# A gated recurrence's output written feature by feature, in quarters of the matmul array

## The chip, the cores and the metric

The kernel runs on one core of a Trainium2 chip. The metric is the device time of one execution in microseconds. A core has a matmul engine (TensorE, PE in the profile, with PEld for its weight loads), three engines for elementwise work (VectorE = DVE, ScalarE = ACT, GpSimd = POOL), and queues from which transfers are issued (SP's above all). Matmul results go to PSUM, in banks of 512 fp32 columns; all else is in SBUF, with 128 partitions.

## The reference

Two stages. The first is a recurrence over 768 time steps for 4 batches and 8 heads of 48 features; the second is a feed-forward layer (MLP) on its output.

```python
f = 1.0 / (1.0 + np.exp(-f_logit))
for t in range(S):
    state = f[:, :, t, :, None] * state + np.einsum('bhd,bhe->bhde', k[:, :, t], v[:, :, t])
    y[:, :, t] = np.einsum('bhd,bhde->bhe', q[:, :, t], state)
x = y.transpose(0, 2, 1, 3).reshape(B * S, H * D)      # 3072 x 384
g = x @ w_gate                                         # 384 x 1536
out = (g / (1 + np.exp(-g)) * (x @ w_val)) @ w_out     # 1536 x 384
```

All inputs and the output are fp32 at the reference; the weights lie in memory as 64-bit floats, which the kernel converts itself.

## The kernel before

Time is cut into NCH = 6 blocks of C = 128 steps. A *unit* is one batch in one block, so there are 24 units, block by block with the four batches inside. Within a unit the recurrence is turned into matmuls. `attention(u)` (line 496) is a generator whose steps are:

- step 0: sigmoid of f, transposed so that features lie on partitions. Heads go in pairs: pair `a` of four has its two heads (`par` 0 and 1) at partitions 0 and 64. In blocks 0 and 1 the transposes are matmuls with an identity (line 505, tiles fTp, kTp, qTp); from block 2 on VectorE does them (lines 511, 531, 532).
- step 1: products of the gates from each step to the block's end (`tail`, a scan on VectorE, line 519), and three small operations.
- step 2: kT scaled by the tails, a second scan (`head`), qT scaled by it (lines 537 to 540), and from block 1 on `decayed`, the carried state times the whole block's decay (line 544), at the end of the step.
- step 3: scores `sc` = k against q (line 552), made causal on VectorE into `A` (line 554); the transpose `kt` of kT (line 559).
- step 4: the output y, and `dS`, the block's addition to the state (line 606), which the last block leaves out.
- step 5: in block 0 alone, the transposes of the output.

The MLP wants its input as `xT`: 384 features in three columns of 128 partitions, 512 tokens (four batches of one block) in the free dimension. Before the change step 4 gets there in two ways. In block 0 y comes out with time on partitions (line 599, eight matmuls), ScalarE copies it to `x`, three transposes (line 619) and a copy (line 620) make `xT`. In blocks 1 to 5 y comes out transposed at once, one head to a half of the array (64 columns): eight matmuls with `decayed` (line 578, 48 rows and 64 columns each) and eight with v and `A` (line 582, 128 rows and 64 columns) into two PSUM banks. Two ScalarE copies make `yT` (line 586), and ten transfers from SBUF to SBUF on SP's queue (line 593) move each head's 48 features to its place in `xT`, ten because heads 2 and 5 straddle two columns of 128.

The MLP has two forms. Block 0's (`mlp_plain`) is done directly, while the weights are loaded in 18 pieces, sized on ScalarE and joined on VectorE (lines 447 to 459). Blocks 1 to 5 (`mlp_fifteen`, `down_seven`) use fewer products with sums made on VectorE; ScalarE copies products out of PSUM (line 841).

What sets the order of the work: block 0's four units run first, in an order written out by hand at the end of `short_path` (`run(b, steps)`), which is kept on TensorE, VectorE and ScalarE. Before them `keep_warm(n)` puts n matmuls on dummy data. Then, for each block c, `take_turns` weaves the pieces of the MLP of block c with the steps of the units of block c + 1 (`attention_steps`); within that a scheduler places each instruction in its engine's queue ahead of time, by its own costs, and each engine runs its queue in order. SP's queue, in order too, carries the loads of f, k, q, v (`load`, two units ahead in blocks 0 and 1 and one ahead later, `load_after`), the weight pieces (`fetches`) and the transfers to `xT`. From block 1 on `later` has three PSUM banks, which go round among sc (two), kt, y (two) and dS.

## Time and profile before

| | us |
|---|---|
| median of 8 executions | 634.02 (632.58 to 635.73) |
| the profiled execution | 633.93 |
| its span | 632.2 |
| TensorE busy | 616.2 (97%) |
| VectorE busy | 500.3 (79%) |
| ScalarE busy | 288.7 (46%) |
| y in blocks 1 to 5: L578, L582 busy (320 instructions each) | 16.3, 23.6 |
| y and its transposes in block 0: L599, x12 transposes of L619 | 7.8, about 0.27 each |
| copies of yT (40) | 14.4 |
| transfers yT to xT (200) | 1.8 each from issue to landing |

The profile records each instruction of one execution with its start, its length and what it waited for. Every fp32 matmul shows as two instructions, each with its weight load. Successive matmuls overlap, so a matmul's length is more than what it adds; the distance between starts is what it adds. Rows of a group give line, engine, operation, output<-inputs, shapes and count; a bracket names the idle time before an instruction and what ended it. The chain of waits follows the work that ended last back through what released it. "issue" is time in which an engine waited for nothing that the profile shows; a letter q after an engine (SPq) means its queue. A stretch's row gives the busy time of each engine between two times and the matmul clock that was granted in it (1.0 is full).

### The profile page before, as it was taken

The numbers are of one execution on the slowest core, as the hardware profiler recorded it, in microseconds if no ns is written. First come the engines' busy times: TensorE is split into PE (matmuls) and PEld (weight loads), VectorE is DVE, ScalarE is ACT, GpSimd is POOL, SyncE is SP. The second block draws the span as 40 slices with busy tenths as digits, with TensorE's granted clock in tenths as the row PEclk, the third lists the DMA queues.
The fourth block names the chain that finished last, engine by engine and source line by source line (L and its number), as shares of the span: only waits on it lengthen the run. The fifth ranks groups of instructions, "written<-read, shape, count | busy, mean of one in ns | idle before, by whom it ended". The sixth has DMA issues, their size and how long they took to land.

```text
span 632.2 us, 10566 instructions
## 1 busy us (share of the span) xinstructions
PE 616.2 (97%) x3894; PEld 498.7 (79%) x3894; DVE 500.3 (79%) x941; ACT 288.7 (46%) x528; POOL 2.9 (0%) x22
## 2 busy tenths in 40 slices
PE   7999999999998999999999999999999999999996
PEld 4954545666777789888889988889988889988896
DVE  5888879968899999579997579998669992557641
ACT  1474655403764731476641265562175540166600
POOL 1000000000000000000000000000000000000000
PEclk8999999999998999999999999999999999999999
DMA  9997474106133122422323402323312210100001
GB/s 176 215 215 231 145 193 137 49 14 178 45 86 97 51 51 53 132 60 64 78 72 86 113 25 70 82 58 91 111 43 51 62 26 8 61 0 1 0 1 54
DMA packets 98395, 51.89 MB, mean 82 GB/s; under 512 B 56864, under 2 KB 92192, under 8 KB 98336
## 3 DMA queue, kind: packets, MB, share of 16 engines
q1 hardware_dynamic: 95024, 46.63, 31.2%
q10 hardware_dynamic: 3312, 4.52, 2.0%
q8 instruction: 32, 0.52, 0.4%
q14 instruction: 27, 0.22, 0.1%
HBM read 42.47 MB, written 4.72 MB: 75 GB/s over the span
## 4 chain that ended last, share of the span: by engine, by line
PE 84%; DVE 7%; DMA 3%; ACT 2%; SPq 2%; issue 2%; DVEq 0%; ACTq 0%
PE o L934 17%; PE A L836 14%; PE B L836 11%; PE gate L666 5%; PE val L666 5%; PE o L690 5%; PE o L836 4%; PE c L836 4%; PE sc L552 4%; PE y L582 3%; PE o L988 3%; PE y L578 2%; PE kt L559 1%; PE dS L606 1%; DVE c L731 1%
## 5 line engine op out<-in xcount | busy, mean ns | idle before, releaser
L934 PE MATMUL o<-w_out,h 128*128 128x192 f32 x360 | 62.6, 330 | 0.6 <-DVE h L853 0.3
L836 PE MATMUL A<-xs,w_both 128*128 128x256 f32 x240 | 62.9, 384 | 0.1
L841 ACT COPY c<-A 128x512 f32<-128x512 f32 x40 | 23.5, 587 | 84.3 <-PE A L836 74.3
L934 PEld LDWEIGHTS o<-w_out,h 128*128 128x128 f32 x360 | 58.1, 190 | 2.5 <-ACT c L951 1.1
L728 DVE TENSOR_TENSOR c<-c,aside 128x512 f32<-128x512 f32 x60 | 41.7, 696 | 18.5 <-ACT aside L841 17.8
L841 ACT COPY aside<-A 128x512 f32<-128x512 f32 x60 | 35.1, 584 | 38.1 <-PE A L836 38.1
L836 PEld LDWEIGHTS A<-xs,w_both 128*128 128x128 f32 x240 | 45.5, 192 | 6.9 <-ACT aside L841 0.4
L853 DVE TENSOR_TENSOR h<-h,c 128x256 f32<-128x256 f32 x100 | 42.2, 433 | 8.2 <-ACT h L852 8.2
L731 DVE TENSOR_TENSOR c<-c,aside 128x512 f32<-128x512 f32 x60 | 41.9, 698 | 2.1 <-ACT aside L841 1.8
L836 PE MATMUL B<-xT,extra 128*128 128x256 f32 x160 | 41.8, 384 | 1.3 <-ACT aside L841 1.2
L852 ACT ACTIVATE h<-c 128x256 f32<-128x256 f32 x100 | 41.7, 419 | 2.1 <-DVE c L728 1.5
L836 PE MATMUL c<-xT,w_both 128*128 128x256 f32 x160 | 42.0, 385 | 0.0
L836 PE MATMUL B<-xs,w_both 128*128 128x256 f32 x160 | 41.8, 384 | 0.0
L836 PE MATMUL A<-xs,extra 128*128 128x256 f32 x160 | 41.1, 379 | 0.0
L934 PE MATMUL o<-ws,h 128*128 128x192 f32 x240 | 41.0, 327 | 0.0
L841 ACT COPY aside<-B 128x512 f32<-128x512 f32 x60 | 35.0, 584 | 10.7 <-PE B L836 10.5
L731 DVE TENSOR_TENSOR c<-o,c 128x512 f32<-128x512 f32 x40 | 27.7, 693 | 14.8 <-PE o L836 13.3
L934 PEld LDWEIGHTS o<-ws,h 128*128 128x128 f32 x240 | 39.1, 190 | 0.2
L554 DVE TENSOR_TENSOR A<-sc,causal 128x512 f32<-128x512 f32 x48 | 31.1, 686 | 5.8 <-PE sc L552 5.8
L836 PEld LDWEIGHTS B<-xT,extra 128*128 128x128 f32 x160 | 29.9, 191 | 6.6 <-ACT aside L841 2.4
L586 ACT COPY yT<-y 128x256 f32<-128x256 f32 x40 | 14.4, 373 | 44.3 <-PE y L582 37.3
L552 PEld LDWEIGHTS sc<-qT,kT 48*128 48x128 f32 x384 | 24.7, 187 | 12.5 <-issue 6.4
(132 smaller groups left out, 1196.8 us busy)
## 6 DMA issues: line engine op xcount, KB each, us to landing
fsquares<-in_f_logit_dram SPq DMA_DIRECT2D x64, 96.0 KB, 2.4
ksquares<-in_k_dram SPq DMA_DIRECT2D x64, 96.0 KB, 2.4
qsquares<-in_q_dram SPq DMA_DIRECT2D x64, 96.0 KB, 2.4
v<-in_v_dram SPq DMA_DIRECT2D x24, 192.0 KB, 3.8
w<-in_moe_w_gate_dram SPq DMA_DIRECT2D x6, 768.0 KB, 4.7
w<-in_moe_w_val_dram SPq DMA_DIRECT2D x6, 768.0 KB, 5.3
w<-in_moe_w_out_dram SPq DMA_DIRECT2D x6, 768.0 KB, 5.0
out_dram<-ob ACTq DMA_DIRECT2D x23, 192.0 KB, 2.6
```

The source lines that it names most:

```text
L552: nc.tensor.matmul(sc[par][:, a * C:(a + 1) * C], lhsT=kT[r, a, :], rhs=qT[r, a, :], start=True, stop=True)
L554: nc.vector.tensor_tensor(A[:, par], sc[par].rearrange("p (a t) -> p a t", t=C), causal.unsqueeze(1).broadcast_to((128, HP, C)), ALU.mult)
L582: nc.tensor.matmul(place(a, par), lhsT=v_[:, 2 * a + par, :], rhs=A[:, par, a, :], start=False, stop=a >= HP - 2, skip_group_check=True)
L666: nc.tensor.matmul(p, lhsT=w[:, i, j * 128:(j + 1) * 128], rhs=xT[c][:, i, :], start=(i == 0), stop=(i == KT - 1))
L690: nc.tensor.matmul(p, lhsT=h[n // 2][:, n % 2 * 2 + b // 2, b % 2 * C:(b % 2 + 1) * C], rhs=w_out[:, j, :], start=(n == 0), stop=(n == NF ...
L728: nc.vector.tensor_tensor(dst, a, b, ALU.add)
L731: nc.vector.tensor_tensor(dst, a, b, ALU.subtract)
L836: nc.tensor.matmul(p[name][:, n, :], lhsT=weights_of[a][:, n, cols], rhs=tokens[b], start=fresh and n == 0, stop=True, skip_group_check=True)
L841: nc.scalar.copy(t, p[name])
L852: nc.scalar.activation(dst, src[:, 0, :], AF.Silu)
L853: nc.vector.tensor_tensor(dst, dst, src[:, 1, :], ALU.mult)
L934: nc.tensor.matmul(p[:, n, :], lhsT=lhsTs[j][:, n * C:(n + 1) * C], rhs=rhs[:, j, :], start=first and j == 0 and n == 0, stop=j == NP - 1, ...
```

## The change

The output now comes out of TensorE in the places that `xT` wants, for every block. The 384 features are 12 pieces of 32. Piece n goes to partitions 32 (n mod 4) onwards, that is to one quarter of the array's columns, and to column n // 4 of one PSUM bank. Three pieces hold a pair of heads (96 features). For the carried state `decayed` is copied by ScalarE (two copies, one for each head of a pair) into `blocks`, a tile with two 48 x 48 blocks on the diagonal and zeros elsewhere, so that one matmul of 128 rows and 32 columns serves each piece. For v, with zeros behind each head's 48 features, `flat` lets a slice of 32 features begin 16 before a head or run 16 past it; a piece that two heads share gets two matmuls. One copy then makes `xT`. The product `decayed` moves ahead of kT's scaling. Step 5 is gone, the transfers to `xT` are gone, and y takes one bank.

With it goes another order of loads at the start: f, k, q of two units, then v of the first; v of each later unit with the loads two ahead; one weight piece with each of the first three units. The warming matmuls before the first scores are 6 instead of 12.

```diff
-    decayed = const.tile([128, HP, W], FP32, tag="decayed", name="decayed")
+    decayed = const.tile([128, HP, D], FP32, tag="decayed", name="decayed")
+    blocks = const.tile([128, HP, 2 * D], FP32, tag="blocks", name="blocks")
+    nc.gpsimd.memset(blocks, 0.0)
...
+        if c:
+            nc.vector.tensor_tensor(decayed, states[b], whole.broadcast_to((128, HP, D)), ALU.mult)
+            for par in range(2):
+                r = rows_of(par)
+                nc.scalar.copy(blocks[r, :, par * D:(par + 1) * D], decayed[r])
         nc.vector.tensor_tensor(kT, kp, pairs(tail, 2)[:, :, 0:C], ALU.mult)
...
-        if c:
-            if c < SQUARES:
-                load_after(u)
-            nc.vector.tensor_tensor(decayed[:, :, 0:D], states[b], whole.broadcast_to((128, HP, D)), ALU.mult)
+        if 0 < c < SQUARES:
+            load_after(u)
...
+        y = bank("y")
+
+        def place(n):
+            return y[Q * (n % 4):Q * (n % 4) + Q, n // 4 * C:(n // 4 + 1) * C]
+
+        per = 2 * D // Q
         if c:
-            y = [bank("y") for _ in range(2)]
...
-            for a in range(HP):
-                for par in range(2):
-                    r = rows_of(par)
-                    nc.tensor.matmul(place(a, par), lhsT=decayed[r, a, :], rhs=qT[r, a, :],
-                                     start=a < 2, stop=False, skip_group_check=True)
-            for par in range(2):
-                for a in range(HP):
-                    nc.tensor.matmul(place(a, par), lhsT=v_[:, 2 * a + par, :], rhs=A[:, par, a, :],
-                                     start=False, stop=a >= HP - 2, skip_group_check=True)
-            yT = att.tile([128, 2, HP // 2 * C], FP32, tag="x", name="yT")
...
-                    nc.sync.dma_start(out=xT[c][f % 128:f % 128 + n, f // 128, b * C:(b + 1) * C],
-                                      in_=yT[r:r + n, par, a // 2 * C:(a // 2 + 1) * C])
...
+            for n in range(DM // Q):
+                nc.tensor.matmul(place(n), lhsT=blocks[:, n // per, n % per * Q:(n % per + 1) * Q], rhs=qT[:, n // per, :],
+                                 start=n < 4, stop=False, skip_group_check=True)
+        flat = v_.rearrange("t h e -> t (h e)")
+        met = {n % 4 for n in range(DM // Q)} if c else set()
+        for par in range(2):
+            for n in range(DM // Q):
+                h = 2 * (n // per) + par
+                at = n * Q - h * D
+                if -Q < at < D:
+                    nc.tensor.matmul(place(n), lhsT=flat[:, W * h + at:W * h + at + Q], rhs=A[:, par, n // per, :],
+                                     start=n % 4 not in met, stop=par == 1 or at + Q <= D, skip_group_check=True)
+                    met.add(n % 4)
+        nc.scalar.copy(xT[c][:, :, b * C:(b + 1) * C], y[:, 0:DM].rearrange("p (a t) -> p a t", t=C))
...
-        if not c:
-            p = bank("xTp")
-            for i in range(KT):
-                nc.tensor.transpose(p[:, i * C:(i + 1) * C], x[:, i * 128:(i + 1) * 128], ident)
...
-        parts = [1, 2, 1, 2]
+        parts = [1, 2, 1, 1]
...
-        load(u)
+        load(u, "fkq")
+    load(0, "v")
...
+    def load_ahead(u):
+
+        if u + NRAW < B:
+            load(u + NRAW, "fkq")
+            load(u + 1, "v")
+        elif u + 1 < B:
+            load(u + 1, "v")
+        if u + 1 < B:
+            fetches.pop(0)()
+        if u + NRAW >= B:
+            load(u + NRAW)
...
-    load_after(0)
+    load_ahead(0)
...
-            keep_warm(12)
+            keep_warm(6)
...
-        load_after(b)
-        if b == 1:
-            for _ in range(2):
-                fetches.pop(0)()
+        load_ahead(b)
```

`load(u, what)` loads only the named inputs; otherwise it is as before.

## The prediction

> **What bounds the kernel now.** I read the page's first part (engine shares), then its chain, then the busy time by stretch, then TensorE's instructions around one attention unit, then the first 42 us of the timeline.

> ```profile
> PE 616.2 (97%) x3894; PEld 498.7 (79%) x3894; DVE 500.3 (79%) x941; ACT 288.7 (46%) x528; POOL 2.9 (0%) x22
> ...
> PE 84%; DVE 7%; DMA 3%; ACT 2%; SPq 2%; issue 2%; DVEq 0%; ACTq 0%
> ```

> TensorE is the bound, and DMA with its queue is 5% of the chain. But a busy share is an average; the stretches say where it holds (columns: PE, PEld, DVE, ACT, POOL busy, granted clock).

> ```profile
> 9.86:13.28 3.41, 3.41 (x10) 1.22 (x9) 1.97 (x5) 0.36 (x1) 0.00 (x0) 0.51 1.24 258
> ...
> 140.00:200.00 60.00, 55.91 (x338) 43.37 (x338) 55.62 (x102) 34.05 (x63) 0.00 (x0) 1.00 0.38 101
> ...
> 201.01:204.42 3.41, 3.41 (x11) 2.79 (x9) 3.41 (x9) 0.59 (x1) 0.00 (x0) 0.51 0.28 54
> 260.00:440.00 180.00, 179.73 (x1260) 155.76 (x1260) 152.21 (x293) 92.54 (x179) 0.00 (x0) 1.00 0.29 72
> ```

> From 260 on TensorE has no gap, so each 0.1 us of matmul added there is 0.1 us of time. From 140 to 200 VectorE is 93% busy and sets the pace; TensorE's additions are half hidden there. Twice the clock was 0.51 for 3.41 us.

> One unit's output, from the timeline of TensorE (start, length, line, count):

> ```profile
> 69.92 0.67 PE L578 MATMUL y<-qT,decayed 48*64 48x128 f32 x16
> 70.52 1.09 PE L582 MATMUL y<-A,v 128*64 128x128 f32 x16
> 71.44 0.62 PE L606 MATMUL dS<-v,kt 128*64 128x48 f32 x16
> 71.99 0.70 PE L666 MATMUL gate<-xT,w_both 128*128 128x512 f32 x1
> ```

> Each matmul is two instructions of 0.27 us. In L582 two column halves work at once: 16 instructions are 8 pairs, and the last starts 1.09 - 0.27 = 0.82 after the first, which is 0.16 for entry and 6 steps of 0.11. In L578 four tiles (two row by two column halves) work at once: last start at 0.40, three steps of which the first is 0.16, then 0.20 until the next shape starts. So a step of the array costs 0.11 us whether two or four tiles share it, and a change of tile shape costs about 0.09 beyond a step.

> At 282 us the next rows show whether a column half must wait for the other:

> ```profile
> 282.16 0.98 PE L582 MATMUL y<-A,v 128*64 128x128 f32 x13
> 282.87 0.32 PE L606 MATMUL dS<-v,kt 128*64 128x48 f32 x3
> 282.98 0.27 PE L582 MATMUL y<-A,v 128*64 128x128 f32 x1
> ```

> Three dS instructions of one half start before the other half's last y. Each column tile has its own line of work.

> The start, from the timeline and the load rate in 40 slices of 1.125 us:

> ```profile
> 8.93 0.66 PE L505 MATMUL fTp<-idf,fraw 128*128 128x128 f32 x4 [1.68 <-DMA fraw<-in_f_logit_dram]
> ...
> 9.42 4.44 PE L360 MATMUL idle<-ones 128*128 128x512 bf16 x12
> 9.48 0.69 DVE L540 TENSOR_TENSOR qT<-qTp,head 128x512 f32<-128x512 f32 x1
> ...
> 11.80 0.18 DVE L524 RECIPROCAL start<-start 128x4 f32<-128x4 f32 x1
> ...
> 13.79 1.16 PE L552 MATMUL sc<-qT,kT 48*128 48x128 f32 x16
> ...
> 15.05 1.29 DVE L554 TENSOR_TENSOR A<-sc,causal 128x512 f32<-128x512 f32 x2 [3.07 <-PE sc L552]
> ...
> GB/s 0 23 207 189 175 164 164 163 163 174 254 389 236 164 165 162 165 170 167 113 123 232 401 388 378 220 175 155 130 172 154 168 174 112 339 338 160 295 391 233
> ```

> VectorE idles 3.07 us because the first scores stand behind twelve warming matmuls, though qT was ready at 10.17. After that VectorE works almost without a gap until 31. One load (196,608 bytes) takes 1.17 us at 165 to 170 GB/s; a weight piece of 786 KB about 2.4.

> **The change, step by step.**

> *Output matmuls, blocks 1 to 5 (20 units).* Gone: 8 matmuls in fours (0.60) and 8 in pairs (0.92, up to dS). New: 12 with the block-diagonal state and 16 with A, all 32 columns wide, 7 per quarter of the array, so 14 instructions in each. If four quarters share a step: 0.16 + 12 x 0.11 = 1.47 until the last starts, 0.20 until the next shape: 1.67 against 1.52, +0.15. The old shape change, L578 to L582, is inside the 1.52; the new one, before dS, costs dS 0.05 more for entry (0.60, as block 0's dS, against 0.55). So +0.20 for each of 16 units, and +0.05 for the last block's 4, which have no dS and left through a shape change before too. Blocks 1, 3 and 4 are paced by TensorE: 12 x 0.20 = 2.4; block 5 0.2; block 2 falls partly in VectorE's stretch, 0.4 of 0.8. Sum +3.0. Bounds: four streams over all 128 rows are shown nowhere (L578's use 48 rows per half, so two streams per row). If only two can run, 28 steps instead of 14: +1.5 a unit. Downward, nothing in the rows beats a 0.11 step, but some units' L578 and L582 were split by other matmuls, each split paying a second entry and exit (0.3): with one PSUM bank instead of two it could get rarer, at most 2 in all. I take +3.0, since L578 is the nearest row.

> [...]

> *The start.* f of unit 1 is fourth in the queue instead of fifth: fTp 1.17 earlier, at 7.76, done 8.2. Six warming matmuls at the old 4.28 / 12 = 0.36 end at 10.3; scores there instead of 13.86. VectorE's small operations end at 11.98, so A begins at 12.0 instead of 15.05: 3.05 won. Later loads eat some: f of unit 3 (twelfth load, after one weight piece) is usable at 4.25 + 11 x 1.17 + 2.4 = 19.5, and VectorE wants its gates at 21.1 with 1.6 of transpose, sigmoid and latencies between: 0 to 0.4 lost. At the end the chain from A (32.67) to the first gate matmul (36.80) was y 1.76, dS 0.60, three transposes 0.55, three times four transposes for the next block 1.3. Now y is about 1.0 and the three are gone, but the weight join on VectorE (0.55 + 0.56 + 0.96 + 0.96 = 3.0 after A) comes level, and q of unit 4 (19th load, three pieces) is usable only at 4.25 + 18 x 1.17 + 7.2 = 32.5. First gate at about 33.4: -3.4. Bounds: -1 (the loads late, or the clock at 0.51 for another 3.41 us after fewer warming matmuls) and -4.5 (no late load). The PE work saved in units 0 to 2 (1.1 each) lies beside VectorE and counts nothing. From there block 0's MLP is TensorE-bound; the second weight join was done 0.7 before its use, a slack that shrinks or stays, worth up to +0.5.

> *200 transfers gone.* 10 a unit at about 0.57 us of SP's queue, 114 us in all, off the path: TensorE ran other pieces meanwhile. The x and q, k, f loads queued behind them start earlier. VectorE waited 3.0 us in total for xT; only one such wait reached TensorE (0.6 at 254.7). I take -0.4; up to -2.

> *ScalarE.* Two copies of 0.373 become one of 0.48 (L602's shape) plus two of about 0.32 (the 192-wide state copy): +0.37 a unit, +7.5 us on an engine at 46%. Covered by TensorE's work; without that cover up to 0.4 a unit. The block copies wait for VectorE's decayed product; behind them in ScalarE's order stand the copies that empty the MLP's banks. I take 0.

> *VectorE.* The decayed product (0.36) moves ahead of the scores' inputs. Same total; where TensorE waits for qT (1.78 at 199.5) it waits 0.36 longer: +0.4. POOL's new memset of 384 columns is before the first v load is needed: 0.

> Sum: +3.0 - 3.4 - 0.4 + 0.4 = -0.4. The profiled execution is 633.93 (span 632.2 and 1.7 around it), the median 634.02: 633.6, which this kernel's spread (0.2%, 1.3 us) can't tell from no change.

> **Rivals.**
> - *Four streams don't fit* (slower). Unshown in any row; L578's fours speak for sharing, its 48 rows leave the doubt. 28 steps: +1.5 x 19 = 29 more: 662. It decides early: over 17 units a step of 0.117 instead of 0.11 already makes the kernel slower by over 0.2%.
> - *ScalarE in the way* (slower). Block copies stuck behind VectorE hold the bank copies; "ACT up <- DVE" waits of 2 us exist in block 0. At 0.3 a unit x 17: 638.7; decides from 0.1 a unit. Against: the product now comes 2.6 us (kT, head, qT) before it is needed.
> [...]
> - *The start wins little*: loads late or the clock low, -1 instead of -3.4: 636.
> - *More waits go than I count* (faster): SP's transfers no longer delay loads between 150 and 200, the 0.51 stretch at 201 (1.7 us lost, set off by a 1.8 us gap) doesn't recur, fewer splits: 630.

> **How the numbers follow.** Forecast 0.40, its own range 632 to 635.5; more waits go 0.22; ScalarE 0.13; start 0.10; four streams 0.08; order 0.07. Faster by over 0.2%: 0.12 of the forecast and 0.21: 0.33. Within: 0.20 and 0.06 from the edges: 0.26. Slower: 0.41. The range runs from 629 to 639.5: it leaves out four streams (0.08) and the tail of the faster case.

> **What would show it.** Right: the new y matmuls start four to a step of 0.11, y to dS takes about 1.67; the first gate matmul at 33 to 34; no gap of TensorE before y after 260. Wrong: steps of 0.2; y instructions waiting on ScalarE's block copy; gaps before the transposes at 18 to 20 on f's load; a 0.51 stretch beyond 13.3.

## The result, and the profile after

The changed kernel takes 631.13 us (median of 13 executions, 630.47 to 632.24), the kernel before 633.84 (37 executions): a ratio of 0.996 with a 95% interval of 0.995 to 0.9971. It is faster by 0.4%, 2.7 us; the forecast was 633.6. The profiled execution of the changed kernel took 633.23 us (span 631.4), 0.7 less than that of before, and this is not a contradiction: an execution is 1.5 to 2 us longer when the matmul clock drops to half for 3.41 us in it, and the profiled one is such a one (granted clock 0.50 at 193.54 to 196.95).

Each execution lists its mean granted clock. One half-clock stretch of 3.41 us costs 1.7 us of matmul and lowers the mean by 1.7 / 632 = 0.003, so a mean of 0.998 or more is taken for an execution without one (roughly: the mean leaves out what precedes the first clock record, and holds a drop behind the last matmul that costs nothing, in before 0.50 from 631.0 on, where the last matmul ends at 626.9; five of before's executions at 0.997 take 632.5 or less). Sorted by that, over all the sets of runs that follow, the profiled executions among them; three executions, two of the kernel before (1275 and 3584 us) and one of a later run (786 us), belong to a slower state and are left out:

| kernel | 0.998 or more | median us | below 0.998 | median us |
|---|---|---|---|---|
| before | 19 of 90 | 631.93 | 71 | 633.98 |
| changed (two sets) | 20 of 27 | 631.08 | 7 | 632.60 |
| loads of the change alone (two sets) | 9 of 24 | 629.99 | 15 | 631.57 |

In before, the 23 with 0.996 or 0.997 and the 48 with 0.995 or less have nearly the same median (634.14 and 633.90), so what its early stretch costs by itself isn't resolved. At equal clock the change is worth 0.85 us. The other two thirds of the 2.7 us are that the clock drops less often, in 7 of 27 executions instead of 71 of 90. That share differs between the two sets of the changed kernel, 1 of 15 and 6 of 12, so the 2.7 depends on the occasion.

The first part of the page and the chain of the changed kernel, by engine:

```profile
PE 612.2 (97%) x4420; PEld 495.0 (78%) x4420; DVE 498.3 (79%) x941; ACT 297.9 (47%) x546; POOL 3.2 (1%) x22
...
PE 78%; DVE 13%; DMA 4%; ACT 3%; issue 2%; SPq 0%; DVEq 0%; ACTq 0%
```

TensorE has 526 instructions more and is 4 us less busy. y with its transposes is busy 45.7 us instead of 49.8, all of it won in block 0 (blocks 1 to 5 alone went from 39.9 to over 41), and the warming 3.8 instead of 6.8; other rows grew, the scores' from 30.3 to 32.0. SP's queue is gone from the chain (it held 2%). Busy time by stretch (PE, PEld, DVE, ACT, POOL busy, then granted clock):

```profile
9.86:13.28 3.42, 2.81 (x28) 2.27 (x28) 3.35 (x8) 0.59 (x1) 0.00 (x0) 1.00 1.52 163
...
140.00:200.00 60.00, 56.37 (x393) 44.17 (x392) 57.70 (x107) 35.52 (x67) 0.00 (x0) 0.97 0.36 95
...
193.54:196.95 3.41, 3.41 (x10) 2.69 (x9) 3.41 (x7) 1.81 (x5) 0.00 (x0) 0.50 0.29 81
260.00:440.00 180.00, 178.46 (x1448) 154.19 (x1447) 149.61 (x290) 97.61 (x185) 0.00 (x0) 1.00 0.24 61
```

The clock is full at 9.86 to 13.28 (it was 0.51). The half-clock stretch of block 1 is still there in this execution, at 193.54.

One unit's output, from TensorE's timeline:

```profile
67.34 0.86 PE L587 MATMUL y<-qT,blocks 128*32 128x128 f32 x24
68.03 1.07 PE L596 MATMUL y<-A,v 128*32 128x128 f32 x32
69.03 0.67 PE L603 MATMUL dS<-v,kt 128*64 128x48 f32 x16
69.63 1.55 PE L655 MATMUL gate<-xT,w_both 128*128 128x512 f32 x3
```

From y to dS it is 69.03 - 67.34 = 1.69 for 56 instructions. The four instructions of a step start 0.0065 apart and the steps 0.109 apart, as the single starts in the trace show. The forecast was 1.67.

The start, on TensorE and VectorE:

```profile
7.76 0.66 PE L513 MATMUL fTp<-idf,fraw 128*128 128x128 f32 x4 [0.49 <-DMA fraw<-in_f_logit_dram]
8.26 1.46 PE L360 MATMUL idle<-ones 128*128 128x512 bf16 x6
...
10.32 1.16 PE L563 MATMUL sc<-qT,kT 48*128 48x128 f32 x16 [0.61 <-DVE qT L553]
...
11.73 1.27 DVE L565 TENSOR_TENSOR A<-sc,causal 128x512 f32<-128x512 f32 x2
...
19.55 0.63 PE L513 MATMUL fTp<-idf,fraw 128*128 128x128 f32 x4 [0.86 <-DMA fraw<-in_f_logit_dram]
...
31.11 0.63 PE L513 MATMUL fTp<-idf,fraw 128*128 128x128 f32 x4 [0.52 <-DMA fraw<-in_f_logit_dram]
...
32.08 0.66 PE L513 MATMUL kTp<-idf,kraw 128*128 128x128 f32 x4 [0.34 <-DMA kraw<-in_k_dram]
...
33.32 0.63 PE L513 MATMUL qTp<-idf,qraw 128*128 128x128 f32 x4 [0.58 <-DMA qraw<-in_q_dram]
...
33.78 5.32 PE L655 MATMUL gate<-xT,w_both 128*128 128x512 f32 x12
```

f of unit 1 is there at 7.76, the scores start at 10.32 (they stood behind warming until 13.79), and the first gate matmul is at 33.78 instead of 36.80, 3.0 earlier. The last three loads before it are each waited for, as the forecast had it for q. The gap at 19.55, which the forecast named as a sign of being wrong, is there (0.86) but held up nothing: VectorE's next scan starts at 20.99, right behind its work before.

### The profile page after: what moved, and what is told of

It is laid out like the page before. It is cut to its first block, busy times and chain, and to the rows that moved or that the text cites. A ratio compares the mean times of both kernels' runs of the same rounds, so it can differ in the third digit from the quotient of the medians.

```text
span 631.4 us, 11292 instructions
## 1 busy us (share of the span) xinstructions
PE 612.2 (97%) x4420; PEld 495.0 (78%) x4420; DVE 498.3 (79%) x941; ACT 297.9 (47%) x546; POOL 3.2 (1%) x22
## 4 chain that ended last, share of the span: by engine, by line
PE 78%; DVE 13%; DMA 4%; ACT 3%; issue 2%; SPq 0%; DVEq 0%; ACTq 0%
PE o L923 17%; PE A L825 13%; PE B L825 11%; PE o L679 5%; PE val L655 5%; PE gate L655 5%; PE o L825 4%; PE c L825 4%; PE sc L563 3%; PE o L977 3%; DVE c L720 2%; PE y L596 2%; PE y L587 2%; DVE h L842 1%; DVE qT L540 1%
## 5 line engine op out<-in xcount | busy, mean ns | idle before, releaser
L830 ACT COPY aside<-B 128x512 f32<-128x512 f32 x60 | 35.1, 585 | 9.8 <-PE B L825 9.6
L720 DVE TENSOR_TENSOR c<-o,c 128x512 f32<-128x512 f32 x40 | 28.1, 703 | 13.2 <-PE o L825 12.7
L825 PEld LDWEIGHTS A<-xs,extra 128*128 128x128 f32 x160 | 30.6, 192 | 6.6 <-ACT c L830 1.3
L599 ACT COPY xT<-y 128x384 f32<-128x384 f32 x24 | 11.5, 478 | 49.7 <-PE y L596 49.7
L825 PEld LDWEIGHTS c<-xT,w_both 128*128 128x128 f32 x160 | 30.8, 194 | 4.7 <-ACT c L830 0.4
```

What stands on the lines that cost most here:

```text
L720: nc.vector.tensor_tensor(dst, a, b, ALU.subtract)
L825: nc.tensor.matmul(p[name][:, n, :], lhsT=weights_of[a][:, n, cols], rhs=tokens[b], start=fresh and n == 0, stop=True, skip_group_check=True)
L830: nc.scalar.copy(t, p[name])
```

## The experiments

All are timed in five rounds beside the kernel before on the same chip. To see where they differ I cut the profiles at the first matmuls of each block's MLP, which also carry the next block's attention (us; the first column is the time of the first gate matmul, the last stage ends at the start of the last matmul, a star marks a stage with a half-clock stretch of 1.7):

| kernel | first gate | block 0 | 1 | 2 | 3 | 4 | 5 |
|---|---|---|---|---|---|---|---|
| before | 36.80 | 112.51 | 104.64* | 98.53 | 97.63 | 93.87 | 82.62 |
| changed, again | 33.62 | 113.36 | 101.24 | 100.09 | 99.09 | 93.56 | 82.57 |
| loads alone | 34.48 | 112.51 | 104.50* | 98.37 | 97.71 | 93.86 | 82.62 |
| loads, and quarters in block 0 | 33.50 | 112.51 | 104.48* | 98.37 | 99.60 | 94.07 | 83.64 |
| quarters alone | 35.17 | 113.46 | 101.33 | 100.08 | 99.09 | 93.56 | 82.57 |
| transfers kept | 33.64 | 113.35 | 102.35 | 99.83 | 99.86 | 94.26 | 83.19 |
| state matmuls twice | 34.09 | 115.98 | 103.79 | 102.17 | 101.73 | 96.18 | 82.57 |

**The changed kernel once more**, with no edit, for its spread and a second profile.

> The changed kernel once more, for a second profiled execution beside the first (633.23, 2.1 us above the median of its timed runs, with one stretch of half clock at 193.5 to 197.0). If that stretch makes the difference, a profile without it should have a span near 629.3 and a time near 631.1, and the place where the span is shorter should be right there, 1.7 us. If the timed median is not about the lost clock, a profile with the stretch can come out at 631 as well.

631.77 (630.78 to 632.66), ratio 0.9976 [0.9961, 0.9991]. The twelve times form two groups: six at 630.78 to 631.10 with a mean clock of 0.998 or more, six at 632.44 to 632.66 with 0.996 or 0.997. This profile (630.8, span 628.9) has no half-clock stretch after its first clock record, at 11.43. Ahead of that it was slow, as the warming matmuls show (2.77 for six instead of 1.46):

```profile
8.77 2.77 PE L360 MATMUL idle<-ones 128*128 128x512 bf16 x6
11.47 1.16 PE L563 MATMUL sc<-qT,kT 48*128 48x128 f32 x16
```

The scores start 1.15 later than in the first profile, and the first gate matmul is at 33.62 all the same: unit 4's loads set it, as the run with the weight pieces last shows. The span is 2.45 shorter than the first profile's, 1.74 of it in block 1's stage, where that one had its half-clock stretch. A median of this kernel thus moves by 1.7 us with the share of either group, which limits what the comparisons below can say; where it matters I use the runs with 0.998 or more.

**The loads alone**: the kernel before with the new order of loads and six warming matmuls.

```diff
-        load(u)
+        load(u, "fkq")
+    load(0, "v")
...
-            keep_warm(12)
+            keep_warm(6)
...
-        load_after(b)
-        if b == 1:
-            for _ in range(2):
-                fetches.pop(0)()
+        load_ahead(b)
```

> The kernel before with the new order of loads and six warming matmuls alone; output matmuls, transfers and transposes as before. Theory (the start carries the gain, the matmuls cost about as much): first gate matmul of the MLP at about 34.5 (3.0 earlier for the scores; the three transposes and the longer y of block 0's last unit stay), time 634 - 2.5 = 631.3. Rival (the start's lead is given back later, by weights or by VectorE's stretch between 140 and 200): the first gate earlier by as much, but time within 0.5 of 633.8.

631.53 (629.68 to 632.3), ratio 0.9958 [0.9943, 0.9973]. And the same kernel on another occasion:

> The kernel before with the new start, once more, as the measure for the next two on the same chip: 631.5 as the first time, with the first gate matmul at 34.47. If its time depends on whether one 3.41 us stretch of half clock falls in (1.7 us), the single times lie in two groups near 630 and 631.7.

631.31 (629.85 to 632.17), ratio 0.996 [0.9947, 0.9972]. The loads alone give as much as the whole change. At full clock they are at 629.99, 1.94 below before and 1.1 below the changed kernel: with these loads the rest of the edit costs 1.1 us net, and what it gives back is that the clock drops less often (7 of 27 against 15 of 24).

**The quarters alone**: the changed kernel with the old order of loads and twelve warming matmuls.

```diff
-        load(u, "fkq")
-    load(0, "v")
+        load(u)
...
-            keep_warm(6)
+            keep_warm(12)
...
-        load_ahead(b)
+        load_after(b)
+        if b == 1:
+            for _ in range(2):
+                fetches.pop(0)()
```

> The changed kernel with the old order of loads and twelve warming matmuls; the new output matmuls alone. Theory of the prediction: +3.0 for the matmuls in blocks 1 to 5, -0.7 at the end of block 0's units (shorter y, no transposes): about 636. Rival (transfers, their queue and the waits behind them were worth more than counted): 633.8 or less, that is, the new matmuls cost nothing net.

632.7 (631.33 to 635.53), ratio 0.999 [0.9972, 1.0007]: no difference that can be told, and 3.3 below what the forecast's terms gave (636); the rival of 633.8 or less holds. The first gate is 1.63 earlier than before, from block 0's shorter output alone; from there on it is as the changed kernel, stage by stage to 0.1 us. In its profile the clock is low only at 9.8 to 13.2, as in before. Both profiles with the old loads have that early stretch (0.51 in before) and none of the twelve with the new loads has it (1.00 in the changed kernel's first), though two of these were slow until 11.4. In block 1 this execution kept the clock; the first profile of the changed kernel lost it there.

**The state's matmuls twice**: the cost of matmul time in blocks 1 to 5.

```diff
-            for n in range(DM // Q):
+            for n in list(range(DM // Q)) * 2:
```

> The changed kernel with the twelve matmuls of the carried state issued twice in each of the 20 units of blocks 1 to 5, so that the state's part of the output counts twice; it prices matmul time itself. Six more steps of 0.109 are 0.65 a unit. If TensorE sets the pace everywhere: +13.1 (20 units). If the four units of block 2 are hidden behind VectorE: +10.5. If matmul time in the MLP's stream is mostly hidden, as a kernel that loses nothing by the new matmuls would suggest: less than half, under 6.

643.51 (643.37 to 643.83), ratio 1.0156 [1.0133, 1.018]. TensorE's timeline, one unit:

```profile
67.21 1.51 PE L588 MATMUL y<-qT,blocks 128*32 128x128 f32 x47
68.53 1.07 PE L598 MATMUL y<-A,v 128*32 128x128 f32 x32
```

The first part takes 1.32 instead of 0.69, 0.63 more for six steps. Over 20 units that is 12.6, and the time rises by 643.65 - 631.08 = 12.6 (runs at full clock). So matmul time added to y counts in full, VectorE's stretch in block 1 included (that stage grows by 2.55, the others by 2.1 to 2.6). A +3.0 would not be hidden behind anything. But the change did not add 3.0. TensorE's time by kind of matmul, from each start to the next one less the idle time, of before and of the changed kernel's second profile (us; "pieces" are stretches of y matmuls without another in between, at least four for four units):

| stage (block whose MLP it is) | 0 | 1 | 2 | 3 | 4 |
|---|---|---|---|---|---|
| y | 6.09 to 6.73 | 8.00 to 7.06 | 6.65 to 7.48 | 6.67 to 7.13 | 6.84 to 6.73 |
| pieces of y | 4 to 4 | 12 to 5 | 7 to 6 | 7 to 5 | 5 to 4 |
| scores | 4.37 to 4.37 | 4.37 to 5.33 | 5.08 to 5.46 | 4.98 to 5.26 | 5.24 to 5.24 |
| TensorE idle | 0 to 0 | 5.34 to 4.15 | 0.58 to 0.78 | 0.13 to 0.73 | 0 to 0 |

In stage 0 no unit's y is cut: 0.64 for four units is 0.16 each, as forecast, and dS costs 0.05 more (2.20 to 2.41 for four). Before, though, other matmuls cut y into 35 pieces, at about 0.24 a cut ((8.00 - 6.09) / 8), and after the change into 24. Over 20 units y grows by 0.9 and dS by 0.1 (9.50 to 9.64). The scores, cut more often, grow by 1.6.

Before, most of the 0.58 in stage 2 was one wait behind the transfers. After the change the idle time of stages 2 and 3 is ScalarE's. ScalarE, then TensorE, of the second profile:

```profile
321.77 0.72 ACT L549 COPY blocks<-decayed 48x192 f32<-48x192 f32 x2 [2.86 <-DVE decayed L546]
322.52 0.48 ACT L940 COPY c<-o 128x384 f32<-128x384 f32 x1
```

```profile
321.76 0.93 PE L563 MATMUL sc<-qT,kT 48*128 48x128 f32 x10
323.05 3.19 PE L923 MATMUL o<-w_out,h 128*128 128x192 f32 x18 [0.36 <-ACT c L940]
```

The copy `c`, which empties a bank for TensorE, stands behind the block copies. Four such waits (0.32, 0.36, 0.27, 0.35) come to 1.3 us; before and the loads alone have none there.

**Quarter by quarter**: the same output matmuls, issued one quarter after the other.

```diff
-            for n in range(DM // Q):
+            for n in sorted(range(DM // Q), key=lambda n: (n % 4, n)):
```

and the matmuls with `A` likewise.

> The changed kernel with the output matmuls issued quarter by quarter of the array's columns (all of quarter 0, then 1, 2, 3) in place of going round. If every quarter has a line of work of its own, deep enough for the whole unit, the steps stay at four instructions in 0.11 and the time stays within 0.5 us. If the line is shallow or the order is strict, the quarters run one after the other: 28 x 2 = 56 passes of 0.11 in place of 14, +4.6 a unit, about +80. In between, the number of instructions that start beside others shows how far ahead the engine looks.

661.62 (661.32 to 662.21), ratio 1.0443 [1.0422, 1.0463]: 30.5 us above the changed kernel, between the two expectations. TensorE's timeline:

```profile
68.69 1.26 PE L587 MATMUL y<-qT,blocks 128*32 128x128 f32 x20
69.69 0.30 PE L595 MATMUL y<-A,v 128*32 128x128 f32 x1
...
70.04 2.11 PE L595 MATMUL y<-A,v 128*32 128x128 f32 x29
72.08 0.67 PE L602 MATMUL dS<-v,kt 128*64 128x48 f32 x16
```

y to dS takes 72.08 - 68.69 = 3.39 instead of 1.69, and 20 x 1.7 = 34 is about the loss (stages 0 to 4 grow by 29, the start by 1.7). The quarters do run beside each other, or it would be 56 steps, but only in part: the first starts, by the order of issue those of quarter 0, are at 68.691, 68.825 and 68.934, and another line begins at 68.940, right behind the third. In the part with `A`, of eight a quarter, the next line begins right behind the fifth (70.145 and 70.151). About two lines at a time is what results, hence twice the length. The order in which the quarters are issued is part of the design. The changed kernel shows that its order 0, 1, 3, 0, 2, 3, 1, 2 costs no step more: A's 32 instructions take 8 steps of 0.109 from 68.03 on, four to a step. In this run, in both parts, a quarter begins when three instructions of the one before it are left.

**The transfers kept**: the new matmuls, but in blocks 1 to 5 a copy of y into a tile of its own, after dS, and ten transfers from there to `xT`.

```diff
+        if c:
+            pre = att.tile([128, H * W], FP32, tag="kt", name="pre")[:, 0:DM].rearrange("p (a t) -> p a t", t=C)
+            nc.scalar.copy(pre, y[:, 0:DM].rearrange("p (a t) -> p a t", t=C))
...
+                    nc.sync.dma_start(out=xT[c][f % 128:f % 128 + m, f // 128, b * C:(b + 1) * C],
+                                      in_=pre[f % 128:f % 128 + m, f // 128, :])
```

> The changed kernel with the new matmuls, but in blocks 1 to 5 ScalarE copies y to a tile of its own and ten transfers of the old sizes move it to the MLP's input, on SP's queue, as before. If the transfers were off the path: within 0.5 of the changed kernel. If their waits and the loads queued behind them mattered: slower, by up to 3 us, with the difference between 145 and 260 and at the block changes, where VectorE waits for the transfers.

635.52 (634.95 to 637.33), ratio 1.0032 [1.0021, 1.0044]; at full clock 635.64, 4.6 above the changed kernel. That is more than the 3 expected. In its profile the stages from block 1 on are together 2.9 longer, the time behind the last matmul is 1.25 longer, and at three block changes TensorE stands still. Its y is cut into 29 pieces and takes 36.6 us, against 24 and 35.1. Its waits, and TensorE's timeline at the change of block 2 to 3:

```profile
DVE xs L728 <- DMA xT<-pre: 4.9, 4, 2.3
...
PEld o L988 <- DVE ob L728: 4.1, 5, 1.2
```

```profile
349.18 1.03 PE L836 MATMUL A<-xs,w_both 128*128 128x256 f32 x4
...
350.97 2.22 PE L988 MATMUL o<-w_out,h 128*128 128x192 f32 x12 [0.77 <-DVE ob L728]
```

The copy is later than the change's and shares the tile of `kt`, so 4.6 is not the price of the transfers in the kernel before. The next run has them where before had them.

**The loads, and quarters in block 0 alone**: blocks 1 to 5 as before, with halves and transfers. Against the changed kernel this leaves the edit of blocks 1 to 5.

```diff
-            for h in range(H):
-                nc.tensor.matmul(y[:, h * D:(h + 1) * D], lhsT=A[:, h % 2, h // 2, :], rhs=v_[:, h, 0:D],
-                                 start=True, stop=True)
-            x = att.tile([128, DM], FP32, tag="x", name="x")
-            nc.scalar.copy(x, y[:, 0:DM])
+            per = 2 * D // Q
...
+            nc.scalar.copy(xT[c][:, :, b * C:(b + 1) * C], y[:, 0:DM].rearrange("p (a t) -> p a t", t=C))
```

> The kernel before with the new start and the new output matmuls in block 0 alone (no transposes there); blocks 1 to 5 keep halves, two copies and transfers. If the gain of the change lies in block 0 and the rest costs as much as it wins: first gate matmul at 33.7 in place of 34.5, and 0.7 us below the kernel with the start alone, so below the changed kernel too: about 630.8. If the end of block 0 is held by the loads of unit 4 and the weight join alone, no gain over the start alone.

631.52 (629.97 to 634.08), ratio 0.9977 [0.9961, 0.9993], no gain over the loads alone, though the first gate is 1.0 earlier; at full clock 631.39 against the changed kernel's 631.08. The edit of blocks 1 to 5, forecast at +3.0, is worth -0.3 here; but the seven times at full clock reach from 629.97 to 633.08, so not even the sign is settled. What this kernel pays shows at the block changes. TensorE, then VectorE:

```profile
348.86 1.03 PE L843 MATMUL A<-xs,w_both 128*128 128x256 f32 x4
...
351.74 2.22 PE L995 MATMUL o<-w_out,h 128*128 128x192 f32 x12 [1.85 <-DVE ob L735]
```

```profile
348.85 0.43 DVE L741 SCALAR_TENSOR_TENSOR xs<-xT 128x256 f32<-128x256 f32 x1 [1.87 <-DMA xT<-yT]
...
349.87 0.55 DVE L735 TENSOR_TENSOR ob<-c,o 128x384 f32<-128x384 f32 x1
...
351.34 0.35 DVE L735 TENSOR_TENSOR ob<-c,o 128x192 f32<-128x192 f32 x1
```

The same place in the changed kernel's second profile:

```profile
348.31 1.03 PE L825 MATMUL A<-xs,w_both 128*128 128x256 f32 x4
349.17 2.11 PE L977 MATMUL o<-w_out,h 128*128 128x192 f32 x12
```

VectorE's token sums `xs` for the next block wait 1.87 us for the last transfers into `xT`. Behind them in VectorE's order stand the sums `ob` that empty the previous block's output banks, and TensorE needs those banks: 1.85 us of standing still, with no name of a transfer on TensorE's row. Counted from where the matmul would have started (in the changed kernel 0.16 before the end of the one ahead), such waits sum in this kernel to 0.47 + 2.01 + 1.13 = 3.6 us; in before to 0.61, with the loads alone to 0.47, with the transfers kept to 2.4, and in every kernel without transfers to nothing. Blocks 3 to 5 of the table show it: 99.60, 94.07 and 83.64 against 97.71, 93.86 and 82.62 with the loads alone. Why the same attention code pays 0.5 in one kernel and 3.6 in another, apart from how the pieces happen to be laid, is open.

**The same with the product early**: `decayed` ahead of kT's scaling, as the change has it.

```diff
+        if c:
+            nc.vector.tensor_tensor(decayed[:, :, 0:D], states[b], whole.broadcast_to((128, HP, D)), ALU.mult)
         nc.vector.tensor_tensor(kT, kp, pairs(tail, 2)[:, :, 0:C], ALU.mult)
```

> The same, with the decayed product moved ahead of kT as in the changed kernel, for the output matmuls of blocks 1 to 5 in halves. In the stretch that VectorE paces (block 1's MLP, 147 to 251 us) the output matmuls' own time was 9.1 us in the kernel before and 7.1 in the changed one. If the product's place is what makes the difference: 2 us less there, and a time near 629. If the transfers or the quarters make it: 9.1 stays, and the time is that of the kernel without the move.

633.42, ratio 1.0009 [0.999, 1.0028]; at full clock 632.69, with the waits at block changes up to 0.85 + 0.70 + 0.92 + 1.57 = 4.0 us. y in block 1's stage stays in 12 pieces (7.93 us instead of 8.00), so the product's place is not what joined them. Without the quarters the early product wins nothing.

**The product late**: the changed kernel with `decayed` and the two block copies at the end of the step.

```diff
-        if c:
-            nc.vector.tensor_tensor(decayed, states[b], whole.broadcast_to((128, HP, D)), ALU.mult)
-            for par in range(2):
...
         nc.vector.tensor_tensor(kT, kp, pairs(tail, 2)[:, :, 0:C], ALU.mult)
...
+        if c:
+            nc.vector.tensor_tensor(decayed, states[b], whole.broadcast_to((128, HP, D)), ALU.mult)
+            for par in range(2):
```

> The changed kernel with the decayed product and ScalarE's two block copies moved back to the end of step 2, behind qT, where the product stood before. If the copies have slack, as counted (2.6 us ahead): within 0.5. If they come late, TensorE waits for ScalarE ahead of the first output matmuls: 0.3 to 0.7 a unit where TensorE sets the pace, 4 to 11 us in all; if the product ahead of kT costs VectorE's stretch something, it gets faster by up to 0.4 for each wait for qT.

634.99 (633.35 to 635.59), ratio 1.0019 [1.0005, 1.0033]: 3.2 to 3.9 above the two sets of the changed kernel, and slower than before. Around 190 us, ScalarE and TensorE of this kernel:

```profile
190.88 0.71 ACT L555 COPY blocks<-decayed 48x192 f32<-48x192 f32 x2 [3.77 <-DVE decayed L552]
191.61 0.58 ACT L830 COPY c<-A 128x512 f32<-128x512 f32 x1
```

```profile
192.25 1.69 PE L825 MATMUL A<-xs,extra 128*128 128x256 f32 x4 [2.62 <-ACT c L830]
```

and of the changed kernel:

```profile
189.63 0.71 ACT L549 COPY blocks<-decayed 48x192 f32<-48x192 f32 x2 [2.08 <-DVE decayed L546]
190.37 0.59 ACT L830 COPY c<-A 128x512 f32<-128x512 f32 x1
```

```profile
191.00 1.13 PE L825 MATMUL A<-xs,extra 128*128 128x256 f32 x4 [0.93 <-ACT c L830]
192.57 0.48 PE L563 MATMUL sc<-qT,kT 48*128 48x128 f32 x2 [0.43 <-DVE qT L553]
```

This is the rival "ScalarE in the way": the block copies wait 3.77 us for VectorE, the copy that empties bank A stands behind them, and TensorE loses 2.62 us in one piece. With the product early it is 0.93. And all 12 executions have a mean clock below 0.998, 7 of them at 0.994 or 0.995, which fits two stretches. So of the 3.2 and more, 0.85 is work (one stretch against one stretch: 633.45 here, 632.60 there) and the rest is clock.

TensorE's busy time in the 3.41 us before the drop, of before, the changed kernel and this one (fences in that order; the clock in these is 0.99 to 1.00, and behind them 0.51, 0.50 and 0.50):

```profile
197.59:201.00 3.41, 1.62 (x21) 1.40 (x21) 3.41 (x8) 1.04 (x3) 0.00 (x0) 0.99 0.80 205
```

```profile
190.13:193.54 3.41, 1.95 (x8) 1.28 (x9) 3.41 (x8) 3.36 (x7) 0.00 (x0) 1.00 0.76 194
```

```profile
189.26:192.67 3.41, 0.79 (x4) 0.39 (x3) 3.41 (x8) 1.74 (x4) 0.00 (x0) 1.00 0.77 204
```

The less TensorE did in it, the more of the executions drop: 12 of 12 at 0.79 us busy, 15 of 24 at 1.59 (the loads alone), 7 of 27 at 1.95. In before it was one gap of 1.78; in the changed kernel the same work leaves 0.93, 0.43 and 0.15 with matmuls between. The second profile of the changed kernel has the same three gaps (0.92, 0.42, 0.17) and no drop. So 1.95 us of work in 3.41 was little enough here to lose the clock, in some executions. The stretches of full clock ahead of a drop are whole multiples of 3.413 us, the length of a half-clock stretch: 187.73 is 55 of them, in before and in the changed kernel, 426.67 in before 125 and 433.49 in the changed kernel 127. On that raster the three gaps of the second profile fall into a stretch with 2.08 us busy, no drop. Whether the place of the gaps on the raster decides between two executions was not tried. The runs show no sharp threshold: the next one lost the clock after 2.01 us busy, and the kernel with quarters in block 0 alone kept it after 1.70, in the 3.41 us from 348.19.

**The weight pieces last**: unit 4's loads ahead of the third weight piece.

```diff
-        if u + 1 < B:
-            fetches.pop(0)()
         if u + NRAW >= B:
             load(u + NRAW)
+        if u + 1 < B:
+            fetches.pop(0)()
```

> The changed kernel with the loads of unit 4 issued ahead of the third weight piece in place of behind it. After the change TensorE waits 0.52 + 0.34 + 0.58 us for f, k and q of unit 4, before the first gate matmul at 33.78, while the first weight join ends at 32.3. If those loads hold the first gate, it comes 1.2 to 1.5 us earlier and the time falls by as much, to about 629.9. If the third piece, landing 4.7 us later, holds the MLP's second gate product, the gain is given back within block 0: time unchanged.

631.97 (631.16 to 633.05), ratio 0.9973 [0.9961, 0.9986]; at full clock 631.22, the changed kernel's 631.08 within its spread. TensorE:

```profile
32.24 5.42 PE L655 MATMUL gate<-xT,w_both 128*128 128x512 f32 x12 [0.33 <-DVE w_both L467]
...
49.11 2.84 PE L655 MATMUL val<-xT,w_both 128*128 128x512 f32 x6 [1.16 <-DVE w_both L467]
```

The first gate comes 1.5 earlier, and block 0's MLP is 1.5 longer, 1.16 of it at 49 us, where the weights are now late. The start is bound by the loads as a whole; one order or the other only moves the wait.

**Twelve warming matmuls**: the changed kernel with the old count.

```diff
-            keep_warm(6)
+            keep_warm(12)
```

> The changed kernel with twelve warming matmuls in place of six, the new order of loads kept. If the earlier f of unit 1 alone keeps the clock full: twelve at 0.22 us end at 10.9, scores 0.6 later, A at 12.3 in place of 11.7; time +0.4 to +0.6. If it was the number of warming matmuls that cost the time: scores near 13.8 as before, +2 or more.

631.18 (630.37 to 632.79), ratio 0.997 [0.9957, 0.9983]; at full clock 630.92. TensorE:

```profile
8.18 2.75 PE L360 MATMUL idle<-ones 128*128 128x512 bf16 x12
10.87 1.16 PE L563 MATMUL sc<-qT,kT 48*128 48x128 f32 x16
```

Twelve now take 2.75 instead of 4.44 (0.23 each, as the changed kernel's six at 1.00 take 0.24; in before, at 0.51 from 9.86, 0.37), and delay the scores by 0.55, which the time doesn't show. What brings the scores forward is the earlier f; the smaller count is worth nothing. This execution lost the clock at a third place, 33.39, after 3.41 us with TensorE busy 1.84 while it waited for f, k and q of unit 4.

## Why the prediction was right or wrong

The time lies in the range, 2.5 us below the forecast and nearest to the rival "more waits go than I count" (630). At equal clock the total, -0.85 against -0.4, is closer than its terms: errors of one and two microseconds cancel, and that is luck. The terms that failed are the output matmuls' (two too large), and ScalarE's and the clock's, both put at nothing.

- *The output matmuls, +3.0.* Right in mechanism and for a unit in one piece: four quarters share a step of 0.109, y to dS is 1.69 (1.67 forecast), dS 0.60. Wrong in size: +1.0 over the 20 units (y 34.25 to 35.13, dS 9.50 to 9.64). The forecast saw the reason, fewer splits, bounded it at 2, and counted none of it. Both chances against the mechanism fall: four streams fit, and the order (0.07) costs nothing, as A's 32 instructions in 8 steps of 0.109 show. By stage, changed against loads alone: block 0's MLP +0.85 (+0.8 forecast), blocks 2's and 3's +1.7 and +1.4 instead of +0.8 each, block 4's -0.3 instead of +0.2. The excess in blocks 2 and 3 is not y's alone: the scores, which the forecast left out (+1.6 in all), and the waits for ScalarE are in it.
- *Block 1's stage, +0.4 for half hidden units and +0.4 for the product.* Wrong: -1.6 without the clock stretches (101.24 against 104.50 - 1.7). Its y falls from 8.00 to 7.06 and its idle time from 5.34 to 4.15. With the transfers kept 1.1 comes back, and y is cut into 8 pieces instead of 5; whether the transfers or the later copy cut it is open.
- *The start, -3.4.* Right: -3.0 and -3.2 at the first gate in two profiles; in the first each step is within 0.4 of its forecast time. Loads alone -2.3, block 0's output alone -1.6; together less than their sum because unit 4's loads then bind. The rival's slow clock came in the second profile, to 11.43, and cost the first gate nothing.
- *The transfers, -0.4.* Right for this pair: 0.6 in before's profile, nothing after. But the waits belong to the arrangement and not to the edit: 3.6 us with the new start and block 0's quarters, where the forecast bounded them at 2.
- *ScalarE, 0.* Wrong by 1.3 in blocks 2 and 3, where the copies that empty banks stand behind the block copies, as the rival had it. The early product does not prevent these; it prevents more in block 1, as the time of 634.99 with the late product shows.
- *VectorE's product, +0.4.* Wrong in sign. Early, it doesn't lengthen TensorE's gap in block 1; it cuts it, since the block copies on ScalarE no longer hold the bank copies as long (2.62 late, 0.93 early).
- *The clock.* The sum left it as it was and named its going only in a rival, at 1.7 us. It is the larger part of the result: at equal clock the change gives -0.85, and the profiled executions, both with a stretch in block 1, differ by -0.7. The rest of -2.7 is stretches that occur less often; how much of it belongs to the one at 9.86 us and how much to block 1's is open. "A 0.51 stretch beyond 13.3", a sign of being wrong, is in the first profile, as it was in before's.

No kernel here clearly beats the changed one: the loads alone are as fast in the median (631.3 and 631.5), faster by 1.1 at full clock, and drop the clock more often.

## What to carry to other kernels

When an edit takes transfers away, count the waits of whoever stands behind their reader in its engine's queue, not only the rows that name a DMA; and size them in the arrangement that the rest of the change makes. Where TensorE has gaps, look at each execution's mean clock before a median is explained: those of 0.9 to 2.6 us here cost themselves and, in some or all of the executions, another 1.7 us. Issue matmuls on column tiles turn by turn: four shared a step here that way (1.69 us from y to dS), and quarter by quarter only about two (3.39). And price short matmuls by the pieces in which they will run: each cut by another shape cost 0.24 us here, and the cuts outweighed most of what the smaller tiles added.
